# First inputs on two DMA queues with lower_bound behind them, and wd of both halves made ahead of the w1 copies

## The chip, the cores and the metric

The kernel runs on one core of one Trainium2 chip. The metric is device microseconds of one execution, lower is better.

## The reference

A gated recurrence over 6,144 steps for four sequences of 256 channels is followed by a maxout layer:

```python
sig = 1.0 / (1.0 + np.exp(-f_logit))
f = lower_bound + (1.0 - lower_bound) * sig
i = 1.0 - f
for t in range(S):
    h = f[:, t] * h + i[:, t] * x[:, t]
    y[:, t] = h
# y becomes x of the second part: 24576 tokens x 256
g = np.maximum(x @ w1, x @ w2)      # 256 -> 1024
out = g @ w_out                     # 1024 -> 256
```

## The kernel before

The kernel uses max(a, b) = a + relu(b - a). So it makes `wd`, the scaled difference of the two weights, for the first layer, and `w13` = w1 @ w_out, for the part that needs no maximum. The second layer is then relu(y @ wd) @ w_out + y @ w13. The scale is 1 - lower_bound (`om`); `nom` is its negative and makes the decay. Tokens are worked on in blocks of 512. Block 0 comes in two halves of 256 tokens, so that the recurrence starts early. The parts that the change touches (cuts marked by `# ...`):

```python
def fetch_first(k):                       # half k of block 0: f, then x, 256 KB each
    nt = TB // 2
    for s in range(2):
        raw = opool.tile([P, nt // P, D], FP32, name="osb")
        nc.sync.dma_start(out=raw[:], in_=...)

def make_wd(g):                           # DVE, two pieces of 0.74 us
    for kc in range(KC):
        nc.vector.scalar_tensor_tensor(out=wd[...], in0=w2n[g][:, kc, :],
            scalar=om[:, kc : kc + 1], in1=w1s[g][:, kc, :], op0=ALU.mult, op1=ALU.subtract)

def turn_w1(g):   ...                     # PE: eight transposes of half of w1 into PSUM
def keep_w1T(g, pt): ...                  # DVE: copies them out, 0.7 us
def make_w13(kc): ...                     # PE: eight matmuls, the last four need w1T of half 1
def first_layer(j, fc): ...               # PE: two matmuls; after each odd fc a ReLU on ScalarE;
                                          # dT has two buffers, each of two fc

nc.sync.dma_start(out=lbc[:], in_=lower_bound.rearrange("(h p) -> p h", p=P))
nc.vector.tensor_copy(out=ident[:], in_=ident_f[:])
# ... om and nom from lbc, on DVE
fetch_first(0)
fetch_first(1)
for g in range(NG):
    fetch_w(g)                            # four DMAs of 512 KB, SyncE's queue
pool_waits(w1n[0][:, 0, 0:1])             # POOL waits for the first weight,
# ...                                     # then fetches w_out and blocks 1, 2, 3, ...
first_bf16(0, 0, nc.vector.tensor_copy)   # casts of block 0, turns, recurrence of both halves
# ...
scale_w1(0); half_w1(0, nc.scalar.copy); make_wd(0)
pt = turn_w1(0)
keep_w1T(0, pt)
scale_w1(1)
for fc in range(4):
    first_layer(0, fc)
half_w1(1, nc.vector.tensor_copy)
make_wd(1)
pt = turn_w1(1)
for fc in range(4, 8):
    first_layer(0, fc)
keep_w1T(1, pt)
# ... turn of block 1, make_w13(0), make_w13(1), second layer of block 0, turn of block 2, ...
```

Note `lower_bound`'s layout: value h*128 + p goes to partition p, so its 1 KB travels as 256 pieces of 4 bytes.

Of the kernel before, what the change touches and what calls it, by code (L numbers as in the profile page):

```python
# [11 lines left out]
ALU = mybir.AluOpType  # L12
AF = mybir.ActivationFunctionType
ENG = mybir.EngineType
P = 128
# [3 lines left out]
def kernel(  # L19
# [10 lines left out]
    nc = tc.nc  # L30
# [82 lines left out]
    def fetch_first(k):  # L113
        nt = TB // 2
        for s in range(2):
            raw = opool.tile([P, nt // P, D], FP32, name="osb")
            nc.sync.dma_start(  # L117
                out=raw[:],
                in_=srcs[s][0, k * nt : (k + 1) * nt, :].rearrange(
                    "(p i) d -> p i d", p=P  # L120
                ),
            )
            raws[k, s] = raw

    def first_bf16(k, s, copy):
        raw = raws[k, s]
        nat = const.tile([P, TB // 2 // P, D], HALF, name=f"nat{k}{s}")
        copy(out=nat[:], in_=raw[:])
        raws[k, s] = nat

    def first_turn(k):
        nt = TB // 2
        for s in range(2):
            dst = ps_o.tile([P, KC, nt // P, P], HALF, name="ps")
            for q in range(nt // P):
                for h in range(KC):
                    nc.tensor.transpose(
                        dst[:, h, q, :],
                        raws[k, s][:, q, h * P : (h + 1) * P],
                        ident[:],  # L140
                    )
            raws[k, s] = dst[:].rearrange("p k i m -> p k m i")
# [211 lines left out]
    def half_w1(g, copy):  # L354
        for kc in range(KC):
            copy(out=w1h[g][:, kc, :], in_=w1s[g][:, kc, :])
# [26 lines left out]
    def keep_w1T(g, pt):  # L383
        nc.vector.tensor_copy(
            out=w1T[:, g * NQ : (g + 1) * NQ, :],
            in_=pt[:].rearrange("p q k d -> p q (k d)"),
        )
# [42 lines left out]
    def first_layer(j, fc):  # L430
        k, g = divmod(fc, KH)
        if fc % 2 == 0:
            dts["d"] = ps_d.tile([P, 2, TB], FP32, name="dT")
        dT = dts["d"]
        for kc in range(KC):
            nc.tensor.matmul(  # L436
                dT[:, fc % 2, :],
                lhsT=wd[:, kc, unit_cols(fc)],
                rhs=y_of(j, kc),
                start=(kc == 0),  # L440
                stop=(kc == KC - 1),
            )
        if fc % 2:
            nc.scalar.activation(  # L444
                out=rts[j, k][:, g - 1 : g + 1, :].rearrange(
                    "p q (i m) -> p q i m", m=P
                ),
                in_=dT[:].rearrange("p q (m i) -> p q i m", m=P),
                func=AF.Relu,
            )  # L450
# [166 lines left out]
        return [runner(s) for s in steps]  # L617

    with tc.manual_schedule():
        nc.sync.dma_start(out=lbc[:], in_=lower_bound.rearrange("(h p) -> p h", p=P))  # L620
        nc.vector.tensor_copy(out=ident[:], in_=ident_f[:])
        nc.vector.tensor_scalar(
            out=om[:], in0=lbc[:], scalar1=-1.0, scalar2=1.0, op0=ALU.mult, op1=ALU.add
        )
        nc.vector.tensor_scalar_add(out=nom[:], in0=lbc[:], scalar1=-1.0)
        fetch_first(0)
        fetch_first(1)
        for g in range(NG):
            fetch_w(g)
        pool_waits(w1n[0][:, 0, 0:1])  # L630
        nc.gpsimd.dma_start(  # L631
            out=wob[:].rearrange("p (g q) c -> p g (q c)", g=NG),
            in_=moe_w_out.rearrange("(g p q) c -> p g (q c)", g=NG, q=NQ),
        )
        for c in range(1, 6):
            for s in range(2):
                fetch(c, s)
        nc.scalar.activation(out=warm[:], in_=om[:, 0:1], func=AF.Sigmoid)
        wt = ps_d.tile([P, 2, 2 * TB], HALF, name="dT")
        for q in range(8):  # L640
            nc.tensor.transpose(wt[:, 0, 0:P], ident[:], ident[:])
        first_bf16(0, 0, nc.vector.tensor_copy)
        first_bf16(0, 1, nc.vector.tensor_copy)
        first_turn(0)
        first_recurrence(0)
        first_bf16(1, 0, nc.scalar.copy)
        first_bf16(1, 1, nc.scalar.copy)
        first_turn(1)
        first_recurrence(1)
        for q in range(24):  # L650
            nc.tensor.transpose(wt[:, 0, 0:P], ident[:], ident[:])
        scale_w1(0)
        half_w1(0, nc.scalar.copy)
        make_wd(0)
        pt = turn_w1(0)
        keep_w1T(0, pt)
        scale_w1(1)
        for fc in range(4):
            first_layer(0, fc)
        half_w1(1, nc.vector.tensor_copy)  # L660
        make_wd(1)
        pt = turn_w1(1)
        for fc in range(4, 8):
            first_layer(0, fc)
        keep_w1T(1, pt)
        steps = turn_steps(1)
        make_w13(0)
        turn(steps[:8])
        gate(1)
        make_w13(1)  # L670
        turn(steps[8:])
        for step in scan_steps(1):
            step()
        cross(4, 5)
        for fc in range(FC):
            if fc == 4:
                turn(turn_steps(2))
                gate(2)
            second_layer(0, fc)
        for step in scan_steps(2):  # L680
            step()
        for step in make_sevens():
            step()
        for fc in range(FC):
            first_layer(1, fc)
        turn(turn_steps(3))
        gate(3)
        early = scan_steps(3)
        for fc in range(FC):
            first_layer(2, fc)  # L690
            second_layer(1, fc)
            if fc < 4:
                early[fc]()
        cross(6)
        scans = {PAIR0: pair_scans(PAIR0)}
        gates = {0: 0, 1: 1, 4: 2, 5: 3}
        order = {
            2: ("decay0", "drive0"),
            3: ("scan00",),
            4: ("scan01",),  # L700
            6: ("decay1",),
            7: ("drive1",),
        }
        for fc in range(FC):
            first_layer(3, fc)
            second_layer(2, fc)
            if fc in gates:
                pair_gate(PAIR0, gates[fc])
            for t in order.get(fc, ()):
                scans[PAIR0][t]()  # L710

        queue, due = [], 0
        for p in range(PAIR0, NPAIR):
            first = p == PAIR0
            more = p + 1 < NPAIR
            seq = [(27, scans[p]["scan10"]), (36, scans[p]["scan11"])]
            if more:
                scans[p + 1] = pair_scans(p + 1)
                seq += [
                    (64, scans[p + 1]["decay0"]),  # L720
                    (66, scans[p + 1]["drive0"]),
                    (70, scans[p + 1]["scan00"]),
                    (84, scans[p + 1]["scan01"]),
                    (112, lambda: sum3(p)),
                    (131, scans[p + 1]["decay1"]),
                    (133, scans[p + 1]["drive1"]),
                ]
            if not first:
                seq += [
                    (9, lambda: sum1(p - 1)),  # L730
                    (18, lambda: sum2(p - 1)),
                    (50, lambda: sum4(p - 1)),
                ]
                queue += sevenths(p - 1)
            seq.sort(key=lambda e: e[0])
            gates = {4: 0, 6: 1, 12: 2, 14: 3} if more else {}
            for slot in range(2 * FC):
                first_layer(2 * p + slot // FC, slot % FC)
                if first and slot % 2:
                    second_layer(2 * p - 1, slot // 2)  # L740
                if p > PAIR0 + 1 or (p == PAIR0 + 1 and slot >= LAG):
                    due += NSEV / (2 * FC)
                    while due >= 1:
                        due -= 1
                        queue.pop(0)()
                if slot == 2 and p + 3 < NPAIR:
                    cross(blocks[2 * p + 6][3])
                if slot in gates:
                    pair_gate(p + 1, gates[slot])
                while seq and seq[0][0] < (slot + 1) * 9:  # L750
                    seq.pop(0)[1]()
        for step in queue:
            step()
        for j in (NBLK - 2, NBLK - 1):
            for slot in range(FC):
                second_layer(j, slot)
# [30 lines left out]
```

## Time and profile before

| before | |
|---|---|
| time | 380.87 us median of the first 3 runs (380.62 to 381.02) |
| the execution that was profiled | 381.55 us, span in the trace 379.8 us |
| PE busy | 369.1 of 379.8 us |
| start of the first-layer matmuls | 11.87 us |

In every run here the time is the trace's span plus 1.8 to 1.9 us. The page of the kernel before begins so (busy us, share of the span and number of instructions of each engine):

```profile
span 379.8 us, 9454 instructions
PE 369.1 (97%) x4076; PEld 279.9 (74%) x4076; DVE 333.0 (88%) x402; ACT 300.3 (79%) x406; POOL 37.5 (10%) x79
```

TensorE (PE) bounds the kernel; from 100 to 370 us it is busy in all 270 us. Only the start is open to a gain. The timeline of the start, before (columns: start us, length us, engine and source line, operation, tiles out<-in, shapes, count; in brackets the idle time of the engine just before, and what ended it; L128 are the casts of block 0, L213 the decay, L436 the first layer, L348 POOL's wait for the first weight):

```profile
...
0.74 0.44 SPq L620 DMA_DIRECT2D lbc<-in_lower_bound_dram  x1
...
1.25 0.45 SPq L117 DMA_DIRECT2D osb<-in_f_logit_dram  x1
...
2.88 0.17 DVE L622 TENSOR_SCALAR om<-lbc 128x2 f32<-128x2 f32 x1 [1.31 <-DMA lbc<-in_lower_bound_dram]
...
4.00 0.43 DVE L128 CAST nat<-osb 128x512 f16<-128x512 f32 x1 [0.88 <-DMA osb<-in_f_logit_dram]
...
5.25 0.43 DVE L128 CAST nat<-osb 128x512 f16<-128x512 f32 x1 [0.82 <-DMA osb<-in_x_dram]
...
5.76 0.48 DVE L213 TENSOR_SCALAR ff<-u,nom 128x256 f16<-128x256 f16 x2
...
8.72 0.28 POOL L348 COPY waited<-r 128x1 f32<-128x1 f32 x1 [7.41 <-DMA r<-in_moe_w_dram]
...
11.87 0.41 PE L436 MATMUL dT<-r,wd 128*128 128x512 f16 x1
...
```

lower_bound is issued first and is used at 2.88. f of the first half is cast at 4.00, x at 5.25, each when its DMA lands. The first decay starts at 5.76. DVE then works on the two recurrences and wd, and the first matmul of the first layer runs at 11.87.

The same timeline, from the first layer to the turn of block 2 (L378 turns w1, L384 copies it to w1T, L392 is make_w13, L180 turns inputs):

```profile
...
12.54 1.70 PE L436 MATMUL dT<-r,wd 128*128 128x512 f16 x7 [0.26 <-DVE wd L360]
...
14.07 0.61 PE L378 MATMUL ps<-ident,S 128*128 128x128 f16 x8
...
15.13 1.70 PE L436 MATMUL dT<-r,wd 128*128 128x512 f16 x7 [0.23 <-DVE wd L360]
...
16.67 1.04 PE L392 MATMUL ps<-wob,w1T 128*128 128x256 f16 x8
...
22.52 0.62 PE L180 MATMUL ps<-ident,xT 128*128 128x128 f16 x8 [0.30 <-DMA xT<-in_x_dram]
...
```

PE waits for wd twice (0.26 and 0.23 us), turns the second half of w1 before fc 4, and runs make_w13 in one piece. At 22.52 it has waited 0.30 us for block 2's x. The chain of waits has that DMA as its last link that isn't PE work (columns: start us, length us, what):

```profile
11.39 11.08 DMA xT<-in_x_dram
...
22.52 0.62 PE ps L180 x8
```

### The profile page before, as it was taken

How to read it: one execution, taken by the hardware profiler on the slowest of the kernel's cores; microseconds unless marked ns; L12 is line 12 of the kernel's file. 1: busy time of each engine (PE TensorE's matmuls, PEld its weight loads, DVE VectorE, ACT ScalarE, POOL GpSimd, SP SyncE). 2: the span in 40 equal slices, each digit the busy share in tenths (PEclk: the TensorE clock that was granted, in tenths of full speed). 3: DMA queues.
4: the chain of work that ended last, by engine and by line, in shares of the span. 5: the costliest groups of instructions: out<-in, count | busy, mean ns of one | idle time of the engine just before them, and what ended most of it. 6: DMA issues, size and time to landing. Idle time of an engine off the chain costs nothing.

```text
span 379.8 us, 9454 instructions
## 1 busy us (share of the span) xinstructions
PE 369.1 (97%) x4076; PEld 279.9 (74%) x4076; DVE 333.0 (88%) x402; ACT 300.3 (79%) x406; POOL 37.5 (10%) x79
## 2 busy tenths in 40 slices
PE   4999999999999999999999999999999999999995
PEld 3677766777777777777777777777777777777784
DVE  4696789999999999999999999999999999999721
ACT  4846788798798888888888887987888888888740
POOL 1500103101201101102011011011011021000000
PEclk9999999999999999999999999999999999999999
DMA  7994999989999999999899999999999999970223
GB/s 249 242 226 98 265 162 256 167 156 289 195 195 276 180 190 251 202 172 285 143 257 190 219 251 278 127 263 223 182 263 212 188 268 211 192 265 3 110 113 113
DMA packets 103389, 77.17 MB, mean 203 GB/s; under 512 B 93554, under 2 KB 94066, under 8 KB 102642
## 3 DMA queue, kind: packets, MB, share of 16 engines
q1 hardware_dynamic: 100514, 51.13, 59.8%
q0 software_dynamic: 2544, 25.17, 34.5%
q8 instruction: 32, 0.52, 0.6%
q10 hardware_dynamic: 288, 0.26, 0.2%
q14 instruction: 11, 0.09, 0.1%
HBM read 53.48 MB, written 48.23 MB: 268 GB/s over the span
## 4 chain that ended last, share of the span: by engine, by line
PE 89%; DMA 4%; DVE 3%; POOL 1%; SPq 1%; ACT 0%; issue 0%
PE ps L605 42%; PE dT L436 41%; PE ps L482 6%; DMA xT<-in_x_dram 3%; DMA r<-in_moe_w_dram 1%; DVE r L230 1%; DVE S L506 1%; SPq L117 0%; PE ps L180 0%; DVE osb L496 0%; DVE v L223 0%; POOL fT L105 0%; DVE ff L213 0%; ACT r L444 0%; POOL wob L631 0%
## 5 line engine op out<-in xcount | busy, mean ns | idle before, releaser
L444 ACT ACTIVATE r<-dT 128x1024 f16<-128x1024 f32 x192 | 195.8, 1022 | 53.2 <-PE dT L436 53.0
L436 PE MATMUL dT<-r,wd 128*128 128x512 f16 x768 | 225.4, 379 | 1.0 <-DVE wd L360 0.5
L605 PEld LDWEIGHTS <-S 128*128 128x128 f16 x1680 | 110.9, 101 | 37.6 <-issue 0.6
L605 PEld LDWEIGHTS <-r 128*128 128x128 f16 x1260 | 87.3, 101 | 36.6
L230 DVE TENSOR_TENSOR_SCAN r<-ff,r,v 128x512 f16<-128x512 f16 x88 | 108.2, 1270 | 0.8
L605 PE MATMUL ps<-t,S 128*128 128x128 f16 x1260 | 97.8, 219 | 0.0
L436 PEld LDWEIGHTS <-wd 128*128 128x128 f16 x768 | 67.6, 113 | 6.4 <-DVE wd L360 1.1
L506 DVE TENSOR_TENSOR S<-r 128x2560 f16<-128x2560 f16 x42 | 62.4, 1485 | 10.1 <-ACT r L444 10.0
L605 PE MATMUL ps<-wob,r 128*128 128x128 f16 x672 | 67.4, 219 | 0.0
L506 DVE TENSOR_TENSOR S<-r,S 128x2560 f16<-128x2560 f16 x42 | 61.9, 1474 | 0.0
L285 ACT ACTIVATE u<-fT 128x512 f16<-128x512 f16 x88 | 56.0, 636 | 1.0 <-DMA fT<-scr 1.0
L213 DVE TENSOR_SCALAR ff<-u,nom 128x512 f16<-128x512 f16 (+1 forms) x98 | 31.3, 346 | 9.7 <-ACT u L207 5.3
L348 POOL CAST waited<-fT 128x1 f32<-128x1 f16 x21 | 10.8, 513 | 279.5 <-DMA fT<-scr 279.5
L605 PE MATMUL ps<-w,r 128*128 128x128 f16 x168 | 36.8, 219 | 0.0
L562 DVE TENSOR_TENSOR osb<-ps,sn 128x512 f32<-128x512 f32 x42 | 28.7, 684 | 6.8 <-ACT osb L560 5.3
L605 PE MATMUL ps<-t,r 128*128 128x128 f16 x420 | 33.4, 219 | 0.0
L605 PE MATMUL ps<-wob,S 128*128 128x128 f16 x336 | 31.4, 219 | 0.0
L223 DVE TENSOR_TENSOR v<-u,xT 128x1024 f16<-128x1024 f16 x44 | 30.1, 684 | 0.2 <-DMA xT<-scr 0.2
L482 PEld LDWEIGHTS <-r 128*128 128x128 f16 x240 | 23.9, 101 | 6.9
L482 PE MATMUL ps<-wob,r 128*128 128x256 f16 x192 | 26.8, 273 | 0.0
L550 ACT COPY sn<-ps 128x512 f32<-128x512 f32 x42 | 24.6, 587 | 1.1 <-PE ps L605 0.9
L560 ACT COPY osb<-ps 128x512 f32<-128x512 f32 x42 | 24.4, 582 | 0.5 <-PE ps L605 0.5
(56 smaller groups left out, 134.8 us busy)
## 6 DMA issues: line engine op xcount, KB each, us to landing
out_dram<-osb SPq DMA_DIRECT2D x47, 512.0 KB, 3.9
scr<-in_f_logit_dram POOLq DMA_DIRECT2D x22, 512.0 KB, 7.4
scr<-in_x_dram POOLq DMA_DIRECT2D x22, 512.0 KB, 10.4
r<-in_moe_w_dram SPq DMA_DIRECT2D x4, 512.0 KB, 6.8
fT<-in_f_logit_dram POOLq DMA_DIRECT2D x3, 256.0 KB, 9.2
xT<-in_x_dram POOLq DMA_DIRECT2D x3, 256.0 KB, 11.1
osb<-in_f_logit_dram SPq DMA_DIRECT2D x2, 256.0 KB, 4.5
osb<-in_x_dram SPq DMA_DIRECT2D x2, 256.0 KB, 4.1
```

What stands on the lines that cost most here:

```text
L213: nc.vector.tensor_scalar(out=ff[:, h, cols], in0=u[:, h, cols], scalar1=nom[:, h : h + 1], scalar2=1.0, op0=ALU.mult, op1=ALU.add,)
L223: nc.vector.tensor_tensor(out=like(v[:, :, cols], xT), in0=like(u[:, :, cols], xT), in1=xT, op=ALU.mult,)
L230: nc.vector.tensor_tensor_scan(out=y_of(j, h), data0=ff[:, h, o : o + TB], data1=v[:, h, o : o + TB], initial=0.0 if t0 == 0 else y_of(j - ...
L285: nc.scalar.activation(out=mids[p + NBLK, "u"][:, h, cols], in_=held[c, 0][:, h, cols], func=AF.Sigmoid, scale=-1.0,)
L436: nc.tensor.matmul(dT[:, fc % 2, :], lhsT=wd[:, kc, unit_cols(fc)], rhs=y_of(j, kc), start=(kc == 0), stop=(kc == KC - 1),)
L444: nc.scalar.activation(out=rts[j, k][:, g - 1 : g + 1, :].rearrange("p q (i m) -> p q i m", m=P), in_=dT[:].rearrange("p q (m i) -> p q i ...
L482: nc.tensor.matmul(ps[:, r, :], lhsT=left, rhs=right, start=(s == 0 and (r == 0 or j == NBLK - 1)), stop=(s == n - 1 and (r == 1 or j == N ...
L506: nc.vector.tensor_tensor(out=t[:], in0=a, in1=b, op=op)
L550: nc.scalar.copy(out=t[:], in_=bank[b][:])
L560: nc.scalar.copy(out=dst, in_=bank[b][:])
L562: nc.vector.tensor_tensor(out=dst, in0=bank[b][:], in1=snap[name][:], op=ALU.add)
L605: nc.tensor.matmul(bank[b][:, i, :], lhsT=a[:, k, cols], rhs=w, start=fresh, stop=after is not None, skip_group_check=True,)
```

## The change

The intent is to start the recurrence sooner: f of the first half leaves before lower_bound, x of the first half goes at the same time on ScalarE's queue, and lower_bound follows x there. Then DVE makes wd of the second half directly after that of the first, so that PE need not wait for wd. The copies of turned w1 and the cast of w1's second half come later, and the second turn of w1 moves behind fc 7.

```diff
-            nc.sync.dma_start(
+            (nc.scalar if s > k else nc.sync).dma_start(
@@
-        nc.sync.dma_start(out=lbc[:], in_=lower_bound.rearrange("(h p) -> p h", p=P))
+        fetch_first(0)
+        nc.scalar.dma_start(out=lbc[:], in_=lower_bound.rearrange("(h p) -> p h", p=P))
         nc.vector.tensor_copy(out=ident[:], in_=ident_f[:])
-        # om and nom on DVE
-        fetch_first(0)
+        nc.scalar.activation(out=warm[:], in_=ident_f[:, 0:1], func=AF.Sigmoid)
         fetch_first(1)
@@
-        nc.scalar.activation(out=warm[:], in_=om[:, 0:1], func=AF.Sigmoid)
@@
         first_bf16(0, 1, nc.vector.tensor_copy)
+        # nom and om on DVE
         first_turn(0)
@@
         pt = turn_w1(0)
-        keep_w1T(0, pt)
         scale_w1(1)
         for fc in range(4):
             first_layer(0, fc)
+        make_wd(1)
         half_w1(1, nc.vector.tensor_copy)
-        make_wd(1)
-        pt = turn_w1(1)
+        keep_w1T(0, pt)
         for fc in range(4, 8):
             first_layer(0, fc)
+        pt = turn_w1(1)
         keep_w1T(1, pt)
```

(The lines `# om and nom on DVE` stand for two instructions, cut here. `warm` is one small sigmoid ahead of the first real one, so that ScalarE's table is loaded early.)

More of the change, by code (lines that the diff above doesn't have):

```diff
@@ L619 @@
     with tc.manual_schedule():
-        nc.sync.dma_start(out=lbc[:], in_=lower_bound.rearrange("(h p) -> p h", p=P))
+        fetch_first(0)
+        nc.scalar.dma_start(out=lbc[:], in_=lower_bound.rearrange("(h p) -> p h", p=P))
         nc.vector.tensor_copy(out=ident[:], in_=ident_f[:])
-        nc.vector.tensor_scalar(
-            out=om[:], in0=lbc[:], scalar1=-1.0, scalar2=1.0, op0=ALU.mult, op1=ALU.add
-        )
-        nc.vector.tensor_scalar_add(out=nom[:], in0=lbc[:], scalar1=-1.0)
-        fetch_first(0)
+        nc.scalar.activation(out=warm[:], in_=ident_f[:, 0:1], func=AF.Sigmoid)
         fetch_first(1)
@@ L643 @@
         first_bf16(0, 1, nc.vector.tensor_copy)
+        nc.vector.tensor_scalar_add(out=nom[:], in0=lbc[:], scalar1=-1.0)
+        nc.vector.tensor_scalar(
+            out=om[:], in0=lbc[:], scalar1=-1.0, scalar2=1.0, op0=ALU.mult, op1=ALU.add
+        )
         first_turn(0)
```

## The prediction

> **What bounds the kernel.** TensorE. The page gives PE 369.1 of 379.8 us busy; the table of stretches 270.00 of 270.00 us between 100 and 370. The chain of waits is PE from 22.5 us to the end. So the change can gain only what PE loses in the first 22.5 us: about 7 us of idle time, most of it before its first layer starts at 11.87 us (timeline).
>
> **What the start waits for.** The input queue. SyncE issues lower_bound (0.74), four 256 KB inputs (0.48 us apart, first at 1.25) and four 512 KB weights. The casts of the first half's f and x start at 4.00 and 5.25 us, of the second half's f at 6.71, each as its DMA lands (list of waits). The DMA share is 1.0 from 3 us. The second half goes cast, turn, sigmoid (ends 8.64), decay, product, scans, wd (from 11.09, 0.74 us a piece), first-layer matmul 11.87. POOL waits for the first weight (8.66), then issues the rest; block 2's x, issued 11.39, lands at 22.48 and holds PE 0.3 us (chain of waits): the last wait of PE that sets the time.
>
> **What the change moves.**
> 1. f of the first half leaves 0.5 us earlier, x at the same time on ScalarE's queue (1 us earlier), later SyncE issues 0.95 earlier. The Trainium skill, "DMA: Bandwidth & Descriptors", "Issuing engines are not separate DMA queues", says both use the same 16 engines and only issue time is saved. The trace agrees that the engines are full from 3 us, so I count the stream's earlier start (0.5) and a little for a steeper ramp: 0.6 us for the second half's f, the weights, and what POOL issues after them. The first half's f gains 0.2 to 0.4, x about 1.3 (it bound nothing by over 0.1).
> 2. lower_bound lands behind x, at 4 to 4.5 us (estimate; 2.1 us alone). Its reader, the first decay, comes at about 5.4. Off the path.
> 3. The table load (1.28 us) moves to about 1.6 to 2.9; the first sigmoid comes at 4.8. Free.
> 4. wd of the second half ahead of the w1 copies: PE's two waits for wd (0.26, 0.23) shrink, but PE now runs fc 4 to 7 before the second turn of w1, and dT has two buffers: fc 4 must wait for the first ReLU. With the start at 11.27, fc 0 to 3 are issued by 13.4, the ReLU runs 12.8 to 13.8 (1.02 each), fc 4 starts at 13.8, fc 6 at 14.8, the turn of w1 ends at 16.2, its copy (0.68) at 16.95, and only then runs the second half of make_w13: it ends near 17.5, as before (17.6). The reorder gives back 0.5 of the 0.6 us.
>
> **Sum.** 0.1 us at make_w13, plus the 0.3 us wait for block 2's x, now there about 0.6 earlier (21.9). Gain 0.4 us of 380.87: 380.5. Run spread before was 0.4. Range 379.8 to 381.1. Faster by over 2%: 0.01; within 2%: 0.98; slower: 0.01.
>
> **What would show it.** First casts at about 3.7 and 4.2; second half's f cast near 6.1; first-layer matmul near 11.3; fc 4 waiting about 0.4 us for a ReLU; make_w13 interrupted by the w1T copy; no wait for block 2's x; PE at block 2's turn 0.3 to 0.5 us earlier, kept to the end.
>
> **What would make it wrong.** lower_bound's 256 small pieces taking turns with 2 KB pieces and landing after 5.5 us, stalling the decay (up to 0.5 slower); two queues slowing f; block 2's x not landing earlier, which pins PE at 22.5 whatever comes before (no gain); a much steeper ramp (gain near 0.9).

## The result

| | time, median | range | ratio to before |
|---|---|---|---|
| before | 380.87 us | 380.62 to 381.02 (4 runs) | |
| changed | 381.58 us | 381.39 to 381.84 (4 runs) | 1.002 (95% interval 1.0003 to 1.0037) |

The changed kernel is slower by 0.7 us. The prediction said 380.5, and at most 381.1. The spans of the changed kernel's four runs are 379.6 to 379.9 us.

The page of the changed kernel:

```profile
span 379.8 us, 9457 instructions
```

That is the span of the first profile of before, too. This is no contradiction: that profile came from an execution of 381.55 us, 0.7 above the median of the kernel before. I had overlooked that. Later profiles of the same kernel (experiment 1) have spans of 378.8, 379.0 and 379.6 us. The timeline of the start, after (L640 makes nom from lower_bound):

```profile
...
0.74 0.41 ACTq L117 DMA_DIRECT2D osb<-in_x_dram  x1
0.74 0.86 SPq L117 DMA_DIRECT2D osb<-in_f_logit_dram  x2
...
1.18 0.45 ACTq L621 DMA_DIRECT2D lbc<-in_lower_bound_dram  x1
...
4.33 0.76 DVE L128 CAST nat<-osb 128x512 f16<-128x512 f32 x2 [2.77 <-DMA osb<-in_f_logit_dram]
...
6.05 0.17 DVE L640 TENSOR_SCALAR nom<-lbc 128x2 f32<-128x2 f32 x1 [0.96 <-DMA lbc<-in_lower_bound_dram]
...
6.33 0.48 DVE L213 TENSOR_SCALAR ff<-u,nom 128x256 f16<-128x256 f16 x2
...
8.50 0.19 POOL L348 COPY waited<-r 128x1 f32<-128x1 f32 x1 [7.20 <-DMA r<-in_moe_w_dram]
...
11.81 0.41 PE L436 MATMUL dT<-r,wd 128*128 128x512 f16 x1 [0.35 <-DVE wd L360]
...
```

f and x both leave at 0.74; DVE casts f at 4.33, and x right behind it. So f came 0.3 us later than before, and x at least 0.5 us earlier. lower_bound, issued at 1.18, came only at 6.02, and DVE waited for it. The first decay starts at 6.33, which is 0.57 us later than before. Two delays add up in this. In all four profiles of the kernel before the decay starts 1.75 or 1.76 us after f's cast, so by f alone it would have started at about 6.09 (an estimate from these numbers): some 0.33 us come from f and 0.24 from lower_bound. The first matmul is at 11.81 against 11.87: nothing was gained.

The same timeline from the first layer on:

```profile
...
12.48 1.70 PE L436 MATMUL dT<-r,wd 128*128 128x512 f16 x7 [0.26 <-DVE wd L360]
...
14.43 1.94 PE L436 MATMUL dT<-r,wd 128*128 128x512 f16 x8 [0.25 <-ACT r L444]
...
16.20 0.61 PE L378 MATMUL ps<-ident,S 128*128 128x128 f16 x8
...
16.65 0.60 PE L392 MATMUL ps<-wob,w1T 128*128 128x256 f16 x4
16.85 0.69 DVE L384 COPY w1T<-ps 128x1024 f16<-128x1024 f16 x1 [1.59 <-PE ps L378]
...
17.60 0.61 PE L392 MATMUL ps<-wob,w1T 128*128 128x256 f16 x4 [0.35 <-DVE w1T L384]
...
```

The first wait for wd stays (0.26 us); the wait before fc 4 is now for a ReLU (0.25 us). The second turn of w1 comes at 16.20, behind fc 7. Its copy by DVE, 16.85 to 17.54, splits make_w13: the first four matmuls run, the other four wait until 17.60. In one piece the eight took 1.04 us; now 1.56 us pass from 16.65 to 18.21. The chain of waits now runs through both places:

```profile
1.18 4.84 DMA lbc<-in_lower_bound_dram
...
16.85 0.70 DVE w1T L384
```

### The profile page after: what moved, and what is told of

Same layout as the page of the kernel before. It is cut to its first block, busy times and chain, and to the rows that moved or that the text cites. A ratio compares the mean times of both kernels' runs of the same rounds, so it can differ in the third digit from the quotient of the medians.

```text
span 379.8 us, 9457 instructions
## 1 busy us (share of the span) xinstructions
PE 368.7 (97%) x4076; PEld 279.7 (74%) x4076; DVE 332.9 (88%) x402; ACT 300.4 (79%) x406; POOL 37.9 (10%) x79
## 4 chain that ended last, share of the span: by engine, by line
PE 91%; DVE 5%; DMA 1%; ACT 1%; issue 0%; ACTq 0%
PE ps L605 42%; PE dT L436 41%; PE ps L482 6%; DVE r L230 1%; DMA lbc<-in_lower_bound_dram 1%; DVE S L506 1%; PE ps L180 1%; DVE v L223 1%; DVE r L264 1%; ACT r L444 1%; DVE ff L213 0%; PE ps L392 0%; DVE wd L360 0%; DVE osb L496 0%; DVE w1T L384 0%
## 5 line engine op out<-in xcount | busy, mean ns | idle before, releaser
L348 POOL CAST waited<-fT 128x1 f32<-128x1 f16 x21 | 12.1, 575 | 279.8 <-DMA fT<-scr 279.8
```

## The experiments

All kernels gave correct results. Four moments of a trace tell what each does: the start of the first decay (line of `ff`), the start of POOL's copy that waits for the first weight, the start of the first first-layer matmul, and the span less the last of these, called the rest. "Ratio" is to runs of the kernel before on the same chip (95% interval). The times are medians; the row of after_again leaves out its one slow run.

| kernel | first decay | first weight | first matmul | span | rest | time; before there | ratio |
|---|---|---|---|---|---|---|---|
| before, first profile | 5.76 | 8.72 | 11.87 | 379.77 | 367.90 | | |
| null_before | 5.84 | 8.99 | 11.80 | 379.00 | 367.20 | 381.14; 380.95 | 1.0005 (0.9992 to 1.0018) |
| before_look1 | 5.79 | 9.09 | 12.20 | 379.64 | 367.44 | 381.41 once; 380.81 | |
| before_look2 | 5.83 | 8.19 | 11.40 | 378.83 | 367.43 | 380.69 once; 380.81 | |
| changed | 6.33 | 8.50 | 11.81 | 379.81 | 368.00 | 381.58; 380.87 | 1.002 (1.0003 to 1.0037) |
| after_again | | | | | | 381.60; 380.95 | 1.0016 (1.0003 to 1.0029) |
| loads_only | 6.10 | 8.31 | 11.59 | 379.03 | 367.44 | 380.81; 380.95 | 0.9994 (0.9982 to 1.0006) |
| reorder_only | 5.80 | 8.48 | 11.41 | 379.40 | 367.99 | 381.28; 380.95 | 1.0024 (1.0003 to 1.0045) |
| turn_between | 6.06 | 8.36 | 11.54 | 378.98 | 367.44 | 381.29; 381.38 | 0.9998 (0.9982 to 1.0014) |
| lbc_first | 6.80 | 8.31 | 12.41 | 379.82 | 367.41 | 382.25; 381.38 | 1.0024 (1.0005 to 1.0043) |
| lbc_alone | 6.11 | 8.63 | 11.78 | 379.38 | 367.60 | 380.71; 381.38 | 0.9986 (0.9972 to 1.0001) |
| lbc_alone_copy_late | 6.09 | 8.26 | 11.57 | 379.59 | 368.02 | 380.34; 381.38 | 0.9982 (0.9965 to 0.9998) |
| after_rows | 6.18 | 7.57 | 11.67 | 379.64 | 367.97 | 381.56; 380.72 | 1.0017 (1.0003 to 1.0030) |
| two_queues_only | 6.91 | 8.34 | 12.40 | 379.86 | 367.46 | 381.68; 380.72 | 1.0021 (1.0006 to 1.0036) |
| rows_copy_late | 5.36 | 7.73 | 10.85 | 377.85 | 367.00 | 381.07; 380.72 | 0.9995 (0.9977 to 1.0013) |
| two_rows_copy_late | 5.45 | 9.26 | 12.26 | 379.28 | 367.02 | 380.90; 380.72 | 0.9995 (0.9979 to 1.0011) |
| rows_again | 5.23 | 9.10 | 12.11 | 379.14 | 367.03 | 380.37; 380.81 | 0.9986 (0.9972 to 1.0000) |
| rows_look | 5.29 | 8.16 | 11.26 | 378.30 | 367.04 | 380.08 once; 380.81 | |

Two regularities of this table carry the argument. First, the rest depends on the order of work: about 367.4 us with the old order (367.41 to 367.60), 368.0 with the changed one, 367.0 with one more order tried below. It doesn't depend on how the loads are issued. (The rest is larger where PE waits once more: for block 2's x in the first profile of before, for block 1's f, landing at 17.5, in lbc_alone_copy_late. It was smaller in null_before, where wd was ready before PE came. The 367.60 of lbc_alone is not explained.)

Second, in all but two of these traces the first matmul comes 0.78 or 0.79 us after DVE starts on wd, so DVE's chain of work holds it. Where DVE goes through without a wait, that is 5.48 or 5.49 us after the first decay (changed, loads_only, turn_between, lbc_alone_copy_late, after_rows, two_queues_only, rows_copy_late). Where DVE has to wait between the two halves for the sigmoid of the second, because that half's inputs landed late, it is 3.20 to 3.22 us after the second decay instead (first profile of before, two_rows_copy_late, rows_again, rows_look; the waits are 0.29, 0.83, 1.27 and 0.37 us). Four more lie 5.57 to 5.67 us after the first decay, with some slack that was not followed up. In null_before and before_look1 PE's turn of w1, which needs the first weight, ends last.

My theories at the outset: R, the reordering costs what the queues gain. Q, the queue part itself costs. S, the 0.7 us lie between launches or after the start.

### 1. null_before, and two more looks at the kernel before

No edit: the kernel before against itself.

> The kernel before against itself. Theory R (the reordered w1 and wd work costs what the queues gain) and theory Q (the queue part itself costs, by the late lower_bound): ratio 1.000 within 0.0005, and a trace whose PE turns block 2 at 21.6 to 22.5 us. Theory S (the 0.7 us is a difference between launches or lies after the start): ratio off 1 by 0.001 or more.

> A third look at the kernel before. The first profile (381.55 us) had PE wait for block 2's x, the second (380.88 us) had not. Typical if it is near 380.9: first-layer matmul 11.4 to 11.9, no wait for block 2's x, span 378.7 to 379.1.

> A fourth look at the kernel before: as the third. If both show the wait for block 2's x and a span of 379.5 or more, the first profile was typical after all.

The ratio of the null is 1.0005, with an interval that holds 1. PE reached block 2's turn at 21.32, a little before the range that was expected, and turned block 2's x without a wait:

```profile
...
21.77 0.61 PE L180 MATMUL ps<-ident,xT 128*128 128x128 f16 x8
...
```

Neither of the two later looks shows the wait for block 2's x either. before_look1, at 381.41 us a slow one, was late because its first weight came at 9.09 and the first matmul at 12.20. So the 0.3 us wait that the prediction wanted to win back occurs in one profile of four. Against S, the null shows no difference, though its interval reaches 1.0018, which is 0.7 us; what speaks more clearly against S is that most of the loss is found at the start (experiments 3 and 5) and comes again (experiment 4).

### 2. loads_only

The changed kernel with w1 and wd in the old order.

```diff
-        make_wd(1)
         half_w1(1, nc.vector.tensor_copy)
-        keep_w1T(0, pt)
+        make_wd(1)
+        pt = turn_w1(1)
         for fc in range(4, 8):
             first_layer(0, fc)
-        pt = turn_w1(1)
         keep_w1T(1, pt)      # and keep_w1T(0, pt) again straight behind turn_w1(0)
```

> Queue part alone, w1 and wd in the old order. R: first-layer matmul at about 11.8 us as in both traces, make_w13 starts near 16.6, PE reaches block 2's turn 0.4 to 0.5 us earlier than in the changed kernel (about 21.7); time 0.0 to 0.3 us below before. Q: as slow as the changed kernel, 0.5 to 0.7 us above before. S: no prediction for the start; time within 0.7 of before either way.

The first matmul is at 11.59, the rest 367.44, the ratio 0.9994. So the queue part alone neither gains nor loses measurably: Q falls as the cause of 0.7 us. But R's hope for a gain isn't met either. PE reached block 2's turn at 21.32, exactly when null_before did.

### 3. reorder_only

The kernel before with only the second part of the change (the last hunk of the diff above).

> Reordering alone, loads as before. R: first-layer matmul at about 11.9 us, PE waits about 0.2 us twice for a ReLU and 0.35 us for the w1T copy in make_w13, block 2's turn starts at 22.1 to 22.3; time 0.3 to 0.6 us above before. Q: within 0.15 us of before.

The rest is 367.99, as in the changed kernel (368.00), against 367.43 and 367.44 in the typical looks at before: the order costs 0.56 us. Its timeline shows the split make_w13:

```profile
...
16.25 0.60 PE L392 MATMUL ps<-wob,w1T 128*128 128x256 f16 x4
...
16.45 0.69 DVE L384 COPY w1T<-ps 128x1024 f16<-128x1024 f16 x1 [1.23 <-PE ps L378]
...
17.19 0.61 PE L392 MATMUL ps<-wob,w1T 128*128 128x256 f16 x4 [0.35 <-DVE w1T L384]
...
```

The time is above that of before (ratio 1.0024; two of its six runs were stragglers of 382.4 and 383.6, the median is 0.33 us above). It is less than 0.56; in the profiled execution the first matmul happened to come early, at 11.41, and how it was in the others isn't known.

### 4. after_again

No edit: the changed kernel again.

> The changed kernel again on the chip of the other three. R: 0.3 to 0.7 us above before, about the sum of the two halves. Q: the same time, but equal to the queue part alone. S: ratio may fall to 1.000.

Its five ordinary runs (381.1 to 382.3, median 381.60) give 1.0016. The loss was repeated. The sixth, the profiled one, took 1,371.6 us; it is told in the last section and used for nothing else.

### 5. turn_between

The changed kernel with the second turn of w1 and its copy between fc 5 and fc 6.

```diff
-        for fc in range(4, 8):
+        for fc in range(4, 6):
             first_layer(0, fc)
         pt = turn_w1(1)
         keep_w1T(1, pt)
+        for fc in range(6, 8):
+            first_layer(0, fc)
```

> The changed kernel with the second turn of w1 and its copy moved between fc 5 and fc 6 of the first layer. Theory R1 (the reorder costs 0.5 us because make_w13 must wait for a w1T copy that follows a turn placed last): the split of make_w13 goes, its two calls run without a wait, PE reaches block 2's turn 0.4 to 0.6 us earlier than in the changed kernel (about 21.6), span 379.2 to 379.4 against 379.8, time about 0.4 us below the changed kernel. Rival R2 (it is the waits for a ReLU before fc 4 and fc 6 that cost): no gain, for both waits stay; span 379.7 or more.

The copy of w1T now runs beside fc 6 and 7, and make_w13 is whole:

```profile
...
15.46 1.03 PE L436 MATMUL dT<-r,wd 128*128 128x512 f16 x4
15.66 0.69 DVE L384 COPY w1T<-ps 128x1024 f16<-128x1024 f16 x1 [0.57 <-PE ps L378]
...
16.33 1.04 PE L392 MATMUL ps<-wob,w1T 128*128 128x256 f16 x8
...
```

The rest falls from 368.00 to 367.44, the span to 378.98, and the ratio to before is 0.9998. R1 held. Against R2, the wait of PE before fc 4 is still there (0.25 us). Before fc 6 there is no wait to be seen, as the turn of w1 now stands there; but fc 4 to 7 took 1.94 us in the changed kernel against 1.90 in lbc_alone_copy_late, so no more than 0.04 us was lost at fc 6. The split of make_w13 (1.56 us against 1.04) is the other 0.52 of the 0.56 us: the w1T copy that stood alone between a turn and the matmuls that need it. The new place of wd on DVE brings nothing by itself, as it turned one of the two waits for wd into a wait for a ReLU and left the other.

### 6. lbc_first, and the theory that replaced mine

loads_only with lower_bound ahead of x on ScalarE's queue.

```diff
-        fetch_first(0)
         nc.scalar.dma_start(out=lbc[:], in_=lower_bound.rearrange("(h p) -> p h", p=P))
+        fetch_first(0)
```

> Queue part alone, with lower_bound ahead of x on the second queue. Theory L (the late lower_bound holds the DVE chain): lower_bound lands at about 2.9 us, the first decay starts at the end of the first sigmoid, near 5.9 instead of 6.1, and the first-layer matmul comes 0.1 to 0.3 us earlier than in the queue part alone (11.3 to 11.5). Rival F (sharing the engines with x delays f, and this is what holds the start): lower_bound lands early and the first-layer matmul stays at 11.6 or later. L and F may both hold: f's cast stays near 4.2 instead of 3.5. Time within 0.3 us of before.

Both theories failed on a number. Even issued first, lower_bound landed at 4.44 us and not at 2.9, x was cast only at 6.18, and the first matmul came at 12.41, later than in any kernel so far (ratio 1.0024). The table of stretches shows why (columns: stretch, its length, busy us of PE, PEld, DVE, ACT, POOL with counts, PE clock, DMA share, GB/s). In lbc_first, while lower_bound's pieces fly:

```profile
3.00:3.50 0.50, 0.00 (x0) 0.00 (x0) 0.00 (x0) 0.24 (x2) 0.00 (x0) 1.00 0.33 67
3.50:4.00 0.50, 0.00 (x0) 0.00 (x0) 0.00 (x0) 0.00 (x0) 0.00 (x0) 1.00 0.76 103
```

In the changed kernel the same slump stands where lower_bound, behind x, is served:

```profile
3.50:4.00 0.50, 0.00 (x0) 0.00 (x0) 0.00 (x0) 0.00 (x0) 0.00 (x0) 1.00 1.06 402
...
4.50:5.00 0.50, 0.19 (x3) 0.20 (x4) 0.50 (x2) 0.00 (x0) 0.00 (x0) 1.00 0.59 79
5.00:5.50 0.50, 0.50 (x7) 0.50 (x6) 0.09 (x1) 0.05 (x1) 0.00 (x0) 1.00 0.48 144
```

This gave theory T: the 256 pieces of 4 bytes, when they run beside a bulk transfer on the other queue, hold both up. They arrive late themselves, and the total falls to 67 and 79 GB/s in one half microsecond and to 103 and 144 in the next, where stretches without them carry about 400.

### 7. lbc_alone and lbc_alone_copy_late

lbc_alone is loads_only with x of the first half back on SyncE's queue, so that only lower_bound uses the second one.

```diff
-            (nc.scalar if s > k else nc.sync).dma_start(
+            nc.sync.dma_start(
```

> Only lower_bound on the second queue; f and x of both halves on SyncE's queue, f first; w1 and wd in the old order. L and F: f lands at 3.4 to 3.7 us, the first decay starts at 5.2 to 5.4 (5.8 before), first-layer matmul at 10.9 to 11.2, PE reaches block 2's turn at 20.8 to 21.0 (21.3 before); span about 378.5; time 0.3 to 0.6 us below before. If something else holds the start (the landing of the first weight): first-layer matmul stays at 11.4 to 11.8 and the time at that of before.

lower_bound took 3.8 us to land and f was cast at 4.35, not at 3.4 to 3.7. The expected gain at the first matmul did not come (11.78): a slump to 63 GB/s at 3.0 to 3.5 us again. The ratio, 0.9986, has an interval that just holds 1.

lbc_alone_copy_late also moves the first w1T copy behind wd of the second half:

```diff
         pt0 = turn_w1(0)
-        keep_w1T(0, pt0)
         ...
         half_w1(1, nc.vector.tensor_copy)
         make_wd(1)
+        keep_w1T(0, pt0)
         pt = turn_w1(1)
```

> As the last, and the first w1T copy moved behind wd of the second half on DVE, the second turn of w1 left ahead of fc 4. DVE theory (the wait for wd before fc 4 is DVE work, of which the 0.7 us w1T copy may come later): wd of the second half starts up to 0.6 us earlier, unless the scaling of w1's second half holds its cast; fc 5 follows fc 4 with 0.3 us less wait; span 0.2 to 0.4 below lbc_alone; time 0.5 to 0.9 us below before. Rival (fc 4 is held by the ReLU): no more than 0.1 below lbc_alone.

fc 5 follows fc 4 without the wait for wd. In its profile this was lost again. Block 1's f landed at 17.5 us and held PE: its turn comes 1.26 us after the start of make_w13, against 0.88 in rows_copy_late. That is 0.4 of the 1.0 us by which the rest lies above that of rows_copy_late; where the other 0.6 went was not followed up. Four of its six runs are at 380.2 to 380.4. The ratio is 0.9982, the only one that lies below 1 with its whole interval (to 0.9998). Later profiles of this order have a rest of 367.0, which is 0.4 below the old one, so the DVE theory held.

### 8. two_queues_only

The kernel before with one edit, x of the first half on ScalarE's queue. lower_bound stays first on SyncE's.

```diff
-            nc.sync.dma_start(
+            (nc.scalar if s > k else nc.sync).dma_start(
```

> The kernel before with only x of the first half moved to the second queue; lower_bound stays first on SyncE, where it flies alone. T: no hole; f lands at about 4.2, x at about 4.2, lower_bound at 2.9 to 3.3; first decay at 5.8 to 6.0 as before, so the first-layer matmul stays at 11.4 to 11.6, span 378.9 to 379.1, time within 0.2 us of before: the second queue alone gains nothing. Rival (two queues slow f): f after 4.5, first-layer matmul after 11.7, slower by 0.2 or more.

By the numbers the rival was met: f after 4.5, the first matmul after 11.7, slower by more than 0.2 us. My reading is that T is right and was applied wrongly: lower_bound no longer flew alone, because x now ran beside it, and f stood behind it in SyncE's queue. The rows of the next experiment speak for this: there f and x, on two queues too but without small pieces, are cast from 4.16. Here lower_bound landed at 4.43 (2.85 before), f was cast at 5.15 (4.0 to 4.1 before), and the first matmul came at 12.40; ratio 1.0021. The stretch at 3.0 us fell to 83 GB/s:

```profile
3.00:3.50 0.50, 0.00 (x0) 0.00 (x0) 0.00 (x0) 0.00 (x0) 0.00 (x0) 1.00 0.62 83
```

In null_before, where the pieces are through before the bulk begins, the same stretch carries 328:

```profile
3.00:3.50 0.50, 0.00 (x0) 0.00 (x0) 0.11 (x2) 0.20 (x1) 0.00 (x0) 1.00 1.00 328
```

### 9. lower_bound as two rows: after_rows, rows_copy_late, two_rows_copy_late

lower_bound is read as two rows of 512 bytes and turned to a column by TensorE.

```diff
-    lbc = const.tile([P, KC], FP32)
+    lrow = const.tile([KC, P], FP32)
-        nc.scalar.dma_start(out=lbc[:], in_=lower_bound.rearrange("(h p) -> p h", p=P))
+        nc.scalar.dma_start(out=lrow[:], in_=lower_bound.rearrange("(h p) -> h p", p=P))
+        lbc = ps_o.tile([P, KC], FP32, name="ps")
+        nc.tensor.transpose(lbc[:], lrow[:], ident_f[0:KC, 0:KC])
```

after_rows does this in the changed kernel.

> The changed kernel, its lower_bound read as two rows of 512 bytes and turned by TensorE (after the first turns), in place of 256 pieces of 4 bytes; the issue keeps its place behind x. Theory T (the tiny pieces themselves hold the bulk queue for about 0.7 us and arrive late): the hole in the bulk transfer near 4.5 to 5.25 us goes; nom is ready at about 6.0 or before; first decay at about 6.1, first weight lands at 7.6 to 8.0 instead of 8.45, first-layer matmul at 11.4 to 11.6; span 0.2 to 0.4 below the changed kernel's 379.8. Rival (lower_bound is late because it stands behind x in its queue): row or pieces alike, it lands near 5.8 and the first-layer matmul stays at 11.8.

The stretch from 4.5 us now carries 340 GB/s (79 before), a smaller dip to 168 stays in the next one, and the first weight is there at 7.57 (8.50). But the first matmul moved only from 11.81 to 11.67, and the time is not lower (381.56). Two lines tell why:

```profile
4.16 0.76 DVE L128 CAST nat<-osb 128x512 f16<-128x512 f32 x2 [2.60 <-DMA osb<-in_f_logit_dram]
...
5.91 0.16 DVE L643 TENSOR_SCALAR nom<-ps 128x2 f32<-128x2 f32 x1 [0.98 <-PE ps L642]
```

f, which shares the engines with x, is hardly earlier than in the changed kernel. And nom waits for the turn of lower_bound on PE, which stands behind the first turns of f and x there; so the first decay, at 6.18, is still 0.26 us behind the 5.92 that f's cast would allow (4.16 and 1.76). The run thus doesn't tell how early the rows landed, and it can't settle the rival about the place behind x. Experiments 6 to 8 say something of that: the pieces took 3.7 to 3.8 us where they were first in their queue, 4.6 to 4.8 behind x. The rest is 367.97, for the order is the changed one.

rows_copy_late is lbc_alone_copy_late with the rows. two_rows_copy_late also puts x of the first half on the second queue.

> lower_bound as two rows alone on the second queue, f and x on SyncE's with f first, the first w1T copy after wd of the second half. T: f lands at 3.4 to 3.7, first decay at 5.2 to 5.4, first-layer matmul at 10.9 to 11.1; PE at block 2's turn at 20.7 to 21.0 unless block 1's f (landing 16 to 17.5) holds it; span 378.2 to 378.7; time 0.4 to 0.8 us below before. Rival (the start is held by the landing of the weights or of block 1's f): no better than the copy moved without the rows, 380.3.

> As the last, with x of the first half on the second queue behind the two rows. If two queues help once no tiny pieces fly: f and x both near 3.8, f of the second half near 4.8, first decay near 5.5; span within 0.2 of the last. If sharing only delays f: 0.1 to 0.3 us slower than the last.

With rows on the second queue, at the place where lbc_alone_copy_late has pieces, the stretch at 3.0 us carries 393 GB/s instead of 79:

```profile
3.00:3.50 0.50, 0.00 (x0) 0.00 (x0) 0.12 (x2) 0.00 (x0) 0.00 (x0) 1.00 1.03 393
```

That is the cleanest pair for T: the same queues, the same order of issue, pieces against rows (DVE also makes nom earlier here, which touches no load). f is cast at 3.60 instead of 4.32, the first decay starts at 5.36, and the first matmul at 10.85:

```profile
...
3.60 0.43 DVE L128 CAST nat<-osb 128x512 f16<-128x512 f32 x1 [0.48 <-DMA osb<-in_f_logit_dram]
...
5.36 0.48 DVE L213 TENSOR_SCALAR ff<-u,nom 128x256 f16<-128x256 f16 x2 [0.67 <-ACT u L258]
...
10.85 0.41 PE L436 MATMUL dT<-r,wd 128*128 128x512 f16 x1
...
```

That execution took 379.63 us, the lowest. The other five took 380.1 to 381.4, so as a whole the kernel is not shown to be faster (0.9995). In two_rows_copy_late f is cast at 3.42: an x that leaves 0.57 us behind f, at 1.31, does not delay it. An x that leaves at the same moment does. In after_rows, which has no small pieces either, f is cast at 4.16, against 3.47 to 3.60 in the three profiles of rows_copy_late, where x follows f on the same queue. In two_rows_copy_late x of the second half landed only at 7.88, and DVE waited 0.83 us for the sigmoid behind it, which held the first matmul.

### 10. rows_again and rows_look

No edit: rows_copy_late again, to see where its slow executions lose the time.

> The kernel of rows_copy_late again, for its profiled execution took 379.63 us and its other five 380.1 to 381.4. Theory P (block 2's x, which POOL fetches, lands late in most executions and holds PE there, however early the first layer starts): a profile of an execution above 380.5 us shows the first-layer matmul at 10.8 to 11.2 as before and PE waiting 0.5 us or more for block 2's x, which lands at 21 to 22.5 instead of 20.4. Rival V (the start itself varies: f or the weights land late): the first-layer matmul itself is late by the difference.

> The same kernel, another look. P: span minus landing of block 2's x constant at about 357.3 where PE waits for it; V: span minus first-layer matmul constant at about 367.0.

Theory P fell: PE waits for block 2's x in none of them. V held: the span less the first matmul is 367.00, 367.03 and 367.04 us in the three, and the start varies with the loads. The second half's x landed at 6.35, 7.72 and 6.78, the first weight 1.32 or 1.33 us after it each time. In rows_again:

```profile
...
5.23 0.48 DVE L213 TENSOR_SCALAR ff<-u,nom 128x256 f16<-128x256 f16 x2 [0.69 <-ACT u L258]
...
7.75 0.62 ACT L128 CAST nat<-osb 128x512 f16<-128x512 f32 x1 [1.05 <-DMA osb<-in_x_dram]
...
8.89 0.48 DVE L213 TENSOR_SCALAR ff<-u,nom 128x256 f16<-128x256 f16 x2 [1.27 <-ACT u L258]
9.10 0.18 POOL L348 COPY waited<-r 128x1 f32<-128x1 f32 x1 [7.79 <-DMA r<-in_moe_w_dram]
...
12.11 0.41 PE L436 MATMUL dT<-r,wd 128*128 128x512 f16 x1
...
```

The first decay is early, as meant, and it no longer matters: ScalarE waits 1.05 us for x of the second half, its sigmoid comes behind that cast, and DVE waits 1.27 us for the sigmoid. So the landing of the second half's inputs sets the start here, and not that of the weights, which follow in the same queue. The ratio is 0.9986, with an interval to 1.0000. A version that beats both kernels is thus likely (380.37 and 380.08 against 380.81 on one chip; 0.9982 for lbc_alone_copy_late), but by little more than the noise. Why the same loads are there up to 1.4 us earlier or later is open.

## Why the prediction was wrong

**Right: the reorder gives back 0.5 us (point 4).** The text foresaw that fc 4 would wait for a ReLU and that make_w13 would be split by the w1T copy. The runs put it at 0.56 us (rest 368.00 against 367.44), and turn_between showed the copy to be nearly all of it (0.52).

**Wrong: 0.6 us of gain from the queues (points 1 and 2).** This is the step that failed. The text placed the first-layer matmul at 11.27. It came at 11.81, against 11.40, 11.80, 11.87 and 12.20 in four executions of before: no gain. Two steps of the text's path to the first decay, which it put at 5.4, went wrong; it came at 6.33.

- "The first half's f gains 0.2 to 0.4": it lost 0.33. The cast was to come at 3.7 and came at 4.33 (4.19 and 4.28 in loads_only and turn_between, which load in the same way), because x left at the same moment on the other queue. after_rows shows the delay without any small pieces (4.16), the three profiles of rows_copy_late show f ahead of x (3.47 to 3.60). The text named this risk ("two queues slowing f") and did not count it.
- "lower_bound lands behind x, at 4 to 4.5 us … Off the path": it landed at 6.02, and the first decay waited for it, by about 0.24 us (0.15 and 0.02 in loads_only and turn_between; estimates from f's cast and 1.76 us). The number of 2.1 us alone was taken from a flight with no bulk on the other queue. With bulk beside it the same DMA took 3.7 to 3.8 us first in its queue and 4.6 to 4.8 behind x. The text named the pieces too as what could make it wrong, at up to 0.5 us, but left the range without it.

The bulk lost as well: the first weight was there at 8.31 to 8.50 in the three kernels that load so, at 7.57 in after_rows without the slump, so the slump at 4.0 to 5.5 us probably ate the stream's earlier start. That is one trace against three, and the loads vary between executions.

The term was mis-sized in a third way. The text took the second half's f as what holds the first matmul, since in the profile that I read it landed at 6.69 us. In the other three looks at before DVE went from the first half's scans to the second decay without a wait. In the changed kernel it did, too: the second half's f landed at 5.17, early enough, and the first matmul stood 5.48 us behind the late first decay.

**Wrong: 0.3 us from the wait for block 2's x.** The wait was real in that one trace, and in the changed kernel it is gone, as predicted (the DMA landed at 20.41). But three other looks at before don't have it. (Where it occurs it costs 0.46 us, not 0.3: the rest is 367.90 against 367.44.) The profiled execution took 381.55 us and the median was 380.87; both numbers were at hand. A saving counted from a slow execution cannot be taken off the median.

**The sum with the measured terms:** 0 from the queues, 0 from block 2's x, 0.56 lost by the order gives 380.87 + 0.56 = 381.4 us; measured were 381.58 and 381.60. The 0.2 us between is within the spread of the runs. In the end PE reached block 2's turn at 22.10, against 21.13 to 21.94 in the four looks at before.

## What to carry to other kernels

Before costing a wait that a profile shows, compare the profiled execution's own time with the median of the timed ones: a wait that makes it slow is perhaps not there in the others. A DMA of many tiny pieces belongs where no bulk transfer flies beside it, or should be read as rows and turned on the chip; its latency alone (2.1 us here) says nothing about its latency beside bulk (3.7 to 3.8). When two loads of one size leave at the same moment on two queues, the one that is needed first may come later than if it went ahead: 0.6 us here. When work is moved "off the wait", ask what follows it: here PE's turn of w1 was put last, and its copy on DVE then stood alone before the matmuls that need it.

## What the Trainium skill lacked or had wrong

- "DMA: Bandwidth & Descriptors", section "Issuing engines are not separate DMA queues", says that DMAs from several engines end on the same 16 DMA engines and that only issue time is saved. The runs agree: f, with x leaving at the same moment on the other queue, was cast at 4.16 to 4.33 us and x right behind it, while f ahead of x on one queue was cast at 3.47 to 3.60; no kernel gained from the second queue as such.
- The same page lacks what tiny pieces on one queue do to a bulk transfer on another. Its section "Queues, rings and completion order" says that each DMA engine takes turns between queues, packet by packet; "Specifications" says that transfers under 512 bytes make the DMA engine read, modify and write. Neither gives a size for this. Here, beside 256 pieces of 4 bytes, the total was down at 62 to 91 GB/s for half a microsecond in seven kernels, against about 400 in later stretches (changed 79, loads_only 62, turn_between 91, lbc_first 67, lbc_alone 63, lbc_alone_copy_late 79, two_queues_only 83), and rows in the same place did not (393). Whether the read-modify-write is the cause was not tested.
- No page that I read tells how much the landing of one and the same load varies between executions: the first 512 KB weight was there at 8.2 to 9.1 us in four looks at the kernel before, and at 7.7 to 9.1 in three at rows_copy_late, where the second half's x moved with it (6.35 to 7.72). That moves the start by more than this whole change does.
- "TensorE: Matmul & The Clock Gate", section "Seeing it yourself", notes, among the caveats on its clock records, that the clock gate was seen stuck at a quarter for over 50 us. One execution of the changed kernel took 1,371.6 us with PE slow all along, a matmul of 128x512 taking 1,103 ns where it takes 379 otherwise, while the granted clock was recorded as 1.0. It may be the same thing, which no run here shows; it was seen once:

```profile
L436 PE MATMUL dT<-r,wd 128*128 128x512 f16 x768 | 731.6, 1103 | 0.0
```
